# Sparse chunk attention and a gated feed-forward layer on one core: the last output tile in two halves of 256 columns, with new ranks for the order of work

## The chip, the cores and the metric

The kernel runs on one core of a Trainium2 chip. The metric is the time of one execution on the device in microseconds (us), as the median of the runs shown; lower is better. A profiled execution gives the trace: its span goes from the first to the last recorded instruction.

## The reference: what is computed

The inputs are q, k and v of shape (4, 8, 768, 64): four batches, eight heads, 768 positions, 64 features. The keys of each head are cut into 24 chunks of 32. For each query and chunk an upper bound of the scores is worked out from the chunk's smallest and largest key values; each query then attends only to the six chunks with the highest bounds, and causally within them. The result is reshaped to 3072 tokens of 512 features and goes through a gated feed-forward layer.

```
k_min, k_max = min, max of each chunk of 32 keys
ub     = sum(maximum(q * k_min, q * k_max))            # one bound per query and chunk
ub     = where(causal, ub, -1e9)
top    = six chunks with the highest ub
scores = (q @ k.T) / 8, kept where chunk in top and key <= query
attn   = softmax(scores) @ v
x      = attn reshaped to (3072, 512)
xn     = x / sqrt(mean(x*x) + 1e-6) * rms_g
out    = (silu(xn @ w_gate) * (xn @ w_val)) @ w_out    # 512 -> 1536 -> 512, float32
```

## The kernel before

**Work.** The kernel handles 16 pairs of heads, four pairs per batch. For each pair, `prep` (L487) loads q and k by SP's DMA queue (L505), transposes them on PE (L525), moves the result out of PSUM with ACT (L297) or DVE (L301), and takes each chunk's minimum and maximum on DVE (L554, L556). Queries are cast to bfloat16 into a buffer `qn` on POOL or DVE (L301). From the seventh pair on, `duo` (L778) computes the bounds for two pairs at once: matmuls on PE (`ub`, L789), evictions, transposes on PE (`up`, L811), the causal mask on DVE (L818), the eight highest values on DVE (L658), and the selection by threshold (L673, L676), which writes one column per chunk into the same `qn` buffer. Then two DMA transposes on SP (`qs<-qn`, L565), one for each head of the pair, bring queries and selection columns together into the layout that the scores read. `scores` (L851) multiplies them with the keys (`sc`, L876), adds a triangular mask (L882), takes the exponential on ACT (L893), masks on POOL (L899), multiplies with v (`av`, L912, 65 columns) and normalises on DVE (L932, L933).

When the four pairs of a batch are done for half of the rows, `norm` (L945) computes the sum of squares (ACT L960 or DVE L963), the root (DVE L973, POOL L981), scales (L989), and transposes the result by a DMA on SP (L1000) or on PE (L1011). `ffn` (L1025) runs for each batch and each half of 384 rows. For each of twelve blocks of 128 hidden features it runs four gate matmuls (L1045), the tanh on ACT (L1052), a combination on DVE (L1058), four value matmuls (L1066), and the product on DVE (`hh`, L1074). Then come three row tiles of 128 rows (`th`): each is projected by twelve matmuls of 128x512 columns into one PSUM bank (`po`, L1086), in three steps of four matmuls; the bank is copied with a factor of 0.5 into SBUF (`poE`, ACT L299 or DVE L303) and stored by a DMA of 256 KB on SP's queue (L1101).

The weights w_gate, w_val and w_out are loaded in two halves of 768 KB each by POOL's DMA queue (L445, L450), and v by the same queue (L481). In the first part of the kernel 88 dummy matmuls on zeros (L346), 48 of 512 columns and 40 of 256, stand in PE's stream.

**Order.** A planner, the class `Order` (L79), decides the order in which each engine gets its instructions while the program is built. Each step is added with the engines that may run it, a planned cost, what it waits for, and the buffers it opens and uses. Buffers come in fixed numbers: eight PSUM banks (`ps`), three output buffers (`ob`), two `qn` buffers, and so on (L235). Whenever an engine is free in the plan, it takes the ready step with the lowest rank. Where a step may run on either of two engines, the one that takes it first has it. A step's rank is the sum of the planned place of its work, an offset for its kind, and a pace times its number within the work; the offsets by kind are in the table `RANK` (L26 to L42), one for the first batch and one for the others, and the places and paces in `TIMES` (L44 to L60). In `TIMES`, `a` entries are the preparations of pairs, `l` their loads, `s` their scores, `n` the normalisations, `f` the feed-forward halves, `w` the weights. The instructions are then written out in the planned order, and each engine works off its queue in that order.

Of the kernel before, what the change touches and what calls it, by code (L numbers as in the profile page):

```python
# [8 lines left out]
FP32 = mybir.dt.float32  # L9
BF16 = mybir.dt.bfloat16  # L10
ALU = mybir.AluOpType
ACT = mybir.ActivationFunctionType
# [12 lines left out]

RANK = (  # L26
    dict(
        av=439.71, dif=-349.0, eps=-276.35, exp=56.9, kC=119.11, kE=221.89, kT=-479.5,
        kload=-91.99, kmn=-561.73, kmx=-221.73, max=-117.69, qC=120.39, qE=644.67, qN=97.14,
        qT=303.27, qX=110.23, qload=17.43, relu=-156.64, root=392.56, sc=392.96, sel=176.91,  # L30
        selC=388.0, selT=-168.59, sq=-325.5, tp=-47.15, tpE=460.17, ub=-387.44, ubE=-1000.64,
        ubm=-238.37, up=-379.03, vload=-360.06, xb=-167.37, xs=293.02,
    ),
    dict(
        av=-243.01, dif=-122.81, eps=-968.41, exp=80.0, gate=-57.45, hh=-33.27, kC=474.21,
        kE=54.78, kT=-28.02, kload=327.35, kmn=571.37, kmx=673.95, mask=-6.85, max=351.72,
        out=-338.93, po=268.25, poE=188.61, qE=-4.14, qN=444.8, qT=271.57, qX=-691.62,
        qload=314.07, relu=202.91, root=-1348.37, sc=-186.72, sel=354.08, sq=285.76, tanh=579.3,
        tg=-259.04, ub=-101.04, ubE=-390.25, ubm=307.49, up=-117.99, val=-52.48, vload=103.56,
        xT=119.23, xb=-299.83, xs=-84.52,  # L40
    ),
)  # L42

TIMES = {  # L44
# [15 lines left out]
}  # L60


# [139 lines left out]
def kernel(  # L202
# [11 lines left out]
    nc = tc.nc  # L214
    P = nc.NUM_PARTITIONS
    B, H, S, D = q.shape
# [5 lines left out]
    DM = H * D  # L222
    DFF = moe_w_gate.shape[1]
    NHT = DFF // P
# [29 lines left out]
    def add(name, engs, occ, rank, *a, **kw):  # L254
        return order.add(name, engs, occ, rank if isinstance(rank, dict) else {"": rank}, *a, **kw)
# [20 lines left out]
    def tile_of(b, shape, dtype, name):  # L276
        pool = ps if b.kind == "ps" else sb
        b.tile = pool.tile(shape, dtype, name=name, tag=f"{b.kind}{b.slot}")
        return b.tile


    def act(n):
        return 0.065 + n * 0.00083

    def dve(n):
        return 0.07 + n * 0.00104
# [40 lines left out]
    wo = const.tile([P, NHT, DM], BF16, name="wo")  # L327
# [3 lines left out]
    def make_ident(e):  # L331
# [7 lines left out]
        out=first[:], in_=ident_f[:, 0:1], func=ACT.Exp), [c_id])  # L339
# [41 lines left out]
    prev = c_id  # L381
    for n in range(4):
        prev = add("e_all", "POOL", 0.82, -80 + n, lambda e, n=n: e_step(n), [prev])
# [43 lines left out]
    def make_tri(e):  # L427
# [10 lines left out]
        out=gains[:], in_=moe_rms_g.rearrange("(o n) -> o n", o=1).to_broadcast([P, DM])),  # L438
# [15 lines left out]
    for part in range(2):  # L454
        a = add("wg", "POOL", 0.8, {f"w{part}": 1.0},
                lambda e, part=part: load_w(part, wg, moe_w_gate), load=1000000)
        b_ = add("wv", "POOL", 0.8, {f"w{part}": 1.0, "w": 1.0},
                 lambda e, part=part: load_w(part, wv, moe_w_val), load=1000000)
# [566 lines left out]
    def ffn(b, c, at, pace):  # L1025
        cols = slice(c * W, (c + 1) * W)
        hhs, hh_done = [], []
        x = [0]

        def step():  # L1030
            x[0] += 1

        def place(kind):
            return rank(at, 1, kind, x[0], pace)

        for ht in range(NHT):
            gp, vp, sg, tg, hh = Buf("ps", "ffn"), Buf("ps", "ffn"), Buf("ff"), Buf("ff"), Buf("hh")
            hs = slice(ht * P, (ht + 1) * P)
            w = c_w[ht // (NHT // 2)]
            step()  # L1040

            def gate(e, gp=gp, hs=hs):
                t = tile_of(gp, [P, W], FP32, "gp")
                for g in range(NP):
                    nc.tensor.matmul(t[:], wg[:, g, hs], XT[b].tile[:, g, cols],  # L1045
                                     start=(g == 0), stop=(g == NP - 1))

            a = add("gate", "PE", 0.652, place("gate"), gate, XTS[b][c] + [w[0]], opens=[gp], uses=[XT[b]])

            def tanh(e, gp=gp, sg=sg):  # L1050
                t = tile_of(sg, [P, W], BF16, "sg")
                nc.scalar.activation(out=t[:], in_=gp.tile[:], func=ACT.Tanh, scale=0.5)  # L1052

            a = add("tanh", "ACT", act(W), place("tanh"), tanh, [a], opens=[sg], uses=[gp])

            def mix(e, gp=gp, sg=sg, tg=tg):
                t = tile_of(tg, [P, W], BF16, "tg")
                nc.vector.scalar_tensor_tensor(out=t[:], in0=sg.tile[:], scalar=1.0,  # L1058
                                               in1=gp.tile[:], op0=ALU.add, op1=ALU.mult)

            a = add("tg", "DVE", dve(W), place("tg"), mix, [a], opens=[tg], uses=[gp, sg])

            def val(e, vp=vp, hs=hs):
                t = tile_of(vp, [P, W], FP32, "vp")
                for g in range(NP):
                    nc.tensor.matmul(t[:], wv[:, g, hs], XT[b].tile[:, g, cols],  # L1066
                                     start=(g == 0), stop=(g == NP - 1))

            step()
            d = add("val", "PE", 0.652, place("val"), val, XTS[b][c] + [w[1]], opens=[vp], uses=[XT[b]])  # L1070

            def mul(e, vp=vp, tg=tg, hh=hh):
                t = tile_of(hh, [P, W], BF16, "hh")
                nc.vector.tensor_tensor(out=t[:], in0=vp.tile[:], in1=tg.tile[:], op=ALU.mult)  # L1074

            hh_done.append(add("hh", "DVE", dve(W), place("hh"), mul, [a, d], opens=[hh], uses=[vp, tg]))
            hhs.append(hh)
        for th in range(3):
            po, ob = Buf("ps", "po"), Buf("ob")
            prev = None  # L1080
            for part in range(3):
                def proj(e, th=th, part=part, po=po):
                    if part == 0:
                        tile_of(po, [P, DM], FP32, "po")
                    for ht in range(part * 4, part * 4 + 4):
                        nc.tensor.matmul(po.tile[:], hhs[ht].tile[:, th * P:(th + 1) * P],  # L1086
                                         wo[:, ht, :], start=(ht == 0), stop=(ht == NHT - 1))

                hs = range(part * 4, part * 4 + 4)
                step()  # L1090
                prev = add("po", "PE", 0.867, place("po"), proj,
                           [prev] + [hh_done[i] for i in hs] + c_wo, opens=[po],
                           uses=[hhs[i] for i in hs])

            def out_(e, po=po, ob=ob):
                t = tile_of(ob, [P, DM], FP32, "osb")
                evict(e, t[:], po.tile[:], 0.5)

            o = add("poE", "", {"ACT": act(512), "DVE": dve(512)}, place("poE"), out_, [prev], opens=[ob], uses=[po])
            r0 = b * S + c * W + th * P  # L1100
            add("out", "SP", 0.55, place("out"), lambda e, r0=r0, ob=ob: nc.sync.dma_start(  # L1101
                out=out[r0:r0 + P, :], in_=ob.tile[:]), [o], uses=[ob])


    pairs = []
    for p in range(NPAIRS):
        c, b = make_pair(p), p // NP
# [51 lines left out]
```

## Time and profile before

| | |
|---|---|
| median of 3 runs | 316.25 us (315.89 to 316.34) |
| profiled execution, its time | 315.79 us |
| profiled execution, its span | 314.0 us |
| granted TensorE clock (mean of the run) | 1.00 |
| first PE work after the start | 1.3 us |

PE is TensorE's matmul stream, PEld its weight loads, DVE VectorE, ACT ScalarE, POOL GpSimd and SP the engine that issues most DMAs. A row of the page's list of groups reads: line, engine, operation, the tile written and the tile read, their shape, the count, then busy time in us and the mean of one in ns, then the idle time in front of them. Rows of a timeline give start and length in us. The lengths of matmuls are modelled and overlap each other; the distance between two starts is what a matmul costs in the stream. The windows view has for each stretch the length, the busy time and number of instructions for PE, PEld, DVE, ACT and POOL, the granted clock, the DMA share and GB/s. In the DMA views each digit is one of 40 equal slices, and the issues give the size and the time from issue to landing.

### The profile page before, as it was taken

What the parts mean: (1) busy time and instruction counts of PE and PEld (TensorE: products, weight loads), DVE (VectorE), ACT (ScalarE), POOL (GpSimd) and SP (SyncE); (2) the same over time, 40 slices, a digit from 0 to 9 for tenths busy, and PEclk for the clock granted to TensorE, in tenths of its full rate; (3) what the DMA queues carried; (4) which work ended last, traced back from release to release, by engine and by line L of the source; (5) the groups of instructions that cost most, each with busy time, mean ns of one, the idle gap of its engine ahead of it and who ended that gap; (6) DMA issues with size and microseconds to landing.
All of it is one profiled execution on the core that took longest, in us unless ns stands there. A gap on an engine that the chain in (4) does not pass through costs nothing.

```text
span 314.0 us, 7640 instructions
## 1 busy us (share of the span) xinstructions
PE 308.6 (98%) x2844; PEld 196.1 (62%) x2844; DVE 230.7 (73%) x654; ACT 194.4 (62%) x420; POOL 100.7 (32%) x157
## 2 busy tenths in 40 slices
PE   7999999999999999999999999999999999999995
PEld 4567877666566775666667565656666645655542
DVE  7699986888988487967986799879464663873530
ACT  5589987863475987478579654344988823333321
POOL 8666534342353564045357300001522220000000
PEclk9999999999999999999999999999999999999999
DMA  8999989989989898979934640002341045001102
GB/s 171 210 190 178 145 108 207 198 114 143 196 86 199 126 179 152 201 164 222 158 79 61 93 102 0 2 2 52 84 94 59 20 118 150 3 0 65 38 22 111
DMA packets 113301, 35.36 MB, mean 113 GB/s; under 512 B 106224, under 2 KB 110064, under 8 KB 113264
## 3 DMA queue, kind: packets, MB, share of 16 engines
q1 hardware_dynamic: 83152, 26.62, 40.9%
q0 software_dynamic: 28512, 7.87, 25.6%
q10 hardware_dynamic: 1600, 0.39, 0.6%
q8 instruction: 22, 0.36, 0.5%
q14 instruction: 15, 0.12, 0.1%
HBM read 28.57 MB, written 6.29 MB: 111 GB/s over the span
## 4 chain that ended last, share of the span: by engine, by line
PE 97%; DMA 1%; ACTq 0%; ACT 0%; issue 0%
PE gp L1045 20%; PE vp L1066 20%; PE po L1086 20%; PE sc L876 12%; PE av L912 7%; PE busy L346 4%; PE pq L525 4%; PE pk L525 3%; PE ub L789 2%; PE ub L731 2%; DMA qnat<-in_q_dram 1%; PE up L811 1%; PE sc L882 1%; PE up L755 1%; PE tp L1011 0%; ACTq L505 0%
## 5 line engine op out<-in xcount | busy, mean ns | idle before, releaser
L893 ACT ACTIVATE pt<-sc 128x512 bf16<-128x512 f32 (+2 forms) x192 | 88.4, 578 | 10.1 <-PE sc L876 5.3
L1052 ACT ACTIVATE sg<-gp 128x384 bf16<-128x384 f32 x96 | 47.7, 500 | 62.7 <-PE gp L1045 60.0
L1066 PE MATMUL vp<-xT,wv 128*128 128x384 bf16 x384 | 77.0, 326 | 0.0
L1045 PE MATMUL gp<-xT,wg 128*128 128x384 bf16 x384 | 76.2, 326 | 0.0
L1086 PE MATMUL po<-wo,hh 128*128 128x512 bf16 x288 | 69.3, 379 | 0.0
L1058 DVE SCALAR_TENSOR_TENSOR tg<-sg,gp 128x384 bf16<-128x384 bf16 x96 | 52.2, 548 | 21.7 <-ACT sg L1052 19.5
L1074 DVE TENSOR_TENSOR hh<-vp,tg 128x384 bf16<-128x384 f32 x96 | 51.8, 551 | 11.1 <-PE vp L1066 7.3
L1045 PEld LDWEIGHTS <-wg 128*128 128x128 bf16 x384 | 36.8, 98 | 24.5 <-issue 1.0
L1066 PEld LDWEIGHTS <-wv 128*128 128x128 bf16 x384 | 36.9, 98 | 24.1
L876 PE MATMUL sc<-qs,ke 128*128 128x128 bf16 (+5 forms) x420 | 51.4, 251 | 0.0
L1086 PEld LDWEIGHTS <-hh 128*128 128x128 bf16 x288 | 27.6, 98 | 27.5
L301 POOL CAST ke<-kt 64x768 bf16<-64x768 f32 x31 | 26.4, 852 | 36.9 <-ACT kt L297 17.0
L876 PEld LDWEIGHTS <-ke 128*128 128x128 bf16 (+1 forms) x420 | 30.3, 97 | 11.3 <-issue 1.6
L899 POOL TENSOR_SCALAR_AFFINE_SELECT pt<-pt 128x512 bf16<-128x512 bf16 (+1 forms) x48 | 24.4, 527 | 37.6 <-ACT pt L893 37.4
L912 PEld LDWEIGHTS <-pt 128*128 128x128 bf16 x672 | 28.8, 98 | 7.7 <-POOL ke L301 0.6
L912 PE MATMUL av<-vx,pt 128*128 128x65 bf16 x672 | 32.6, 193 | 0.0
L299 ACT ACTIVATE osb<-po 128x512 f32<-128x512 f32 x19 | 11.4, 602 | 21.4 <-PE po L1086 21.4
L346 PE MATMUL busy<-zeros 128*128 128x512 bf16 (+1 forms) x88 | 20.1, 349 | 1.3 <-DVE zeros L341 1.3
L933 DVE TENSOR_TENSOR xb<-av,rden 128x384 bf16<-128x384 f32 (+1 forms) x34 | 18.1, 534 | 1.2
L989 DVE SCALAR_TENSOR_TENSOR xs<-xb,ri,gains 128x512 bf16<-128x512 bf16 x24 | 16.9, 746 | 2.7 <-DMA xT<-xs 2.1
L301 POOL CAST qn<-qnat 128x768 bf16<-128x768 f32 x10 | 8.2, 821 | 31.9 <-DMA qs<-qn 30.7
L481 POOL DMA_DIRECT2D vx<-in_v_dram x16 | 16.8, 1052 | 4.0 <-PE av L912 2.6
(87 smaller groups left out, 303.1 us busy)
## 6 DMA issues: line engine op xcount, KB each, us to landing
out_dram<-osb SPq DMA_DIRECT2D x24, 256.0 KB, 2.2
knat<-in_k_dram SPq DMA_DIRECT2D x30, 192.0 KB, 4.3
qnat<-in_q_dram SPq DMA_DIRECT2D x30, 192.0 KB, 4.8
vx<-in_v_dram POOLq DMA_DIRECT2D x16, 192.0 KB, 4.7
wg<-in_moe_w_gate_dram POOLq DMA_DIRECT2D x2, 768.0 KB, 8.6
wv<-in_moe_w_val_dram POOLq DMA_DIRECT2D x2, 768.0 KB, 7.8
wo<-in_moe_w_out_dram POOLq DMA_DIRECT2D x2, 768.0 KB, 9.9
qs<-qn SPq DMA_TRANSPOSE x26, 3.3
```

The source lines that it names most:

```text
L301: engine[e].tensor_copy(out_, in_)
L346: nc.tensor.matmul(t[:, 0:n], zeros[:, 0:P], zeros[:, 0:n], start=True, stop=True)
L876: nc.tensor.matmul(t[:, x:x + m, :].rearrange("p a b -> p (a b)"), ke[kk, kb * P:(kb + 1) * P], qs[kk, q0 * P:(q0 + m) * P], start=not tri ...
L893: nc.scalar.activation(out=t[:, 0:nn, :], in_=sc.tile[:, 0:nn, :], func=ACT.Exp, scale=SCALE)
L899: nc.gpsimd.affine_select(out=pt.tile[:, 0:nd, :], in_=pt.tile[:, 0:nd, :], compare_op=ALU.is_ge, fill=0.0, base=0, pattern=[[0, nd], [1, ...
L912: nc.tensor.matmul(av.tile[:, qi - i0, :], pt.tile[:, x, :], VX[c.v.slot][:, hl * NT + kb, :], start=(begin and m == 0), stop=(left[0] == ...
L1045: nc.tensor.matmul(t[:], wg[:, g, hs], XT[b].tile[:, g, cols], start=(g == 0), stop=(g == NP - 1))
L1052: nc.scalar.activation(out=t[:], in_=gp.tile[:], func=ACT.Tanh, scale=0.5)
L1058: nc.vector.scalar_tensor_tensor(out=t[:], in0=sg.tile[:], scalar=1.0, in1=gp.tile[:], op0=ALU.add, op1=ALU.mult)
L1066: nc.tensor.matmul(t[:], wv[:, g, hs], XT[b].tile[:, g, cols], start=(g == 0), stop=(g == NP - 1))
L1074: nc.vector.tensor_tensor(out=t[:], in0=vp.tile[:], in1=tg.tile[:], op=ALU.mult)
L1086: nc.tensor.matmul(po.tile[:], hhs[ht].tile[:, th * P:(th + 1) * P], wo[:, ht, :], start=(ht == 0), stop=(ht == NHT - 1))
```

## The change

Two things change. First, in the last feed-forward half (batch 3, second half) the third row tile is no longer projected as one tile of 512 columns but as two of 256 columns. Each has a PSUM buffer of its own, three steps of four matmuls with 256 columns (planned cost 0.44 instead of 0.867), an eviction of 256 columns and a store of 128 KB; the store's rows are half as long. Second, every number in `RANK` and `TIMES` is another, so that the planner writes out another order for all engines, and for steps that may run on either of two engines also another share. The lines from there on move down by two (L1086 becomes L1088, L1101 becomes L1103).

In the changed order, the number of dummy matmuls is the same (88, all in the first part). Of the evictions of output tiles, ACT has 22 and DVE 3, where they had 19 and 5; there are 25 stores instead of 24 and 2306 weight-load instructions instead of 2294 in PE's program. DVE has 8 sums of squares instead of 9, and casts of queries move from POOL (10 to 8) to DVE (3 to 5). On POOL's queue the loads of w_out and v in the middle of the kernel come as w_out, w_out, v, v, v, where they came as v, w_out, v, w_out. The last two tiles on PE are the two halves, whose steps alternate.

```diff
 RANK = (
     dict(
-        av=439.71, dif=-349.0, eps=-276.35, exp=56.9, kC=119.11, kE=221.89, kT=-479.5,
...
+        av=466.73, dif=-380.72, eps=-422.75, exp=-49.4, kC=465.82, kE=55.35, kT=-458.36,
...
 TIMES = {
-    "a0": -417.11, "a1": 120.7, "a10": 211.74, "a11": -52.39, "a12": 226.13, "a13": 390.87,
...
+    "a0": -366.84, "a1": 132.4, "a10": -301.15, "a11": -280.78, "a12": 112.6, "a13": 171.18,
...
-        for th in range(3):
+        last = b == B - 1 and c == 1
+        for th, c0, cn in [(th, c0, DM >> (last and th == 2)) for th in range(3)
+                           for c0 in ((0, DM // 2) if last and th == 2 else (0,))]:
             po, ob = Buf("ps", "po"), Buf("ob")
             prev = None
             for part in range(3):
-                def proj(e, th=th, part=part, po=po):
+                def proj(e, th=th, part=part, po=po, c0=c0, cn=cn):
                     if part == 0:
-                        tile_of(po, [P, DM], FP32, "po")
+                        tile_of(po, [P, cn], FP32, "po")
                     for ht in range(part * 4, part * 4 + 4):
                         nc.tensor.matmul(po.tile[:], hhs[ht].tile[:, th * P:(th + 1) * P],
-                                         wo[:, ht, :], start=(ht == 0), stop=(ht == NHT - 1))
+                                         wo[:, ht, c0:c0 + cn], start=(ht == 0), stop=(ht == NHT - 1))
...
-                prev = add("po", "PE", 0.867, place("po"), proj,
+                prev = add("po", "PE", 0.867 if cn == DM else 0.44, place("po"), proj,
...
-            def out_(e, po=po, ob=ob):
-                t = tile_of(ob, [P, DM], FP32, "osb")
+            def out_(e, po=po, ob=ob, cn=cn):
+                t = tile_of(ob, [P, cn], FP32, "osb")
                 evict(e, t[:], po.tile[:], 0.5)
...
-                out=out[r0:r0 + P, :], in_=ob.tile[:]), [o], uses=[ob])
+                out=out[r0:r0 + P, c0:c0 + cn], in_=ob.tile[:]), [o], uses=[ob])
```

More of the change, by code (lines that the diff above doesn't have):

```diff
@@ L27 @@
     dict(
-        av=439.71, dif=-349.0, eps=-276.35, exp=56.9, kC=119.11, kE=221.89, kT=-479.5,
[L29 to L32, printed above, removed]
+        av=466.73, dif=-380.72, eps=-422.75, exp=-49.4, kC=465.82, kE=55.35, kT=-458.36,
+        kload=-100.05, kmn=-524.02, kmx=-272.62, max=-206.54, qC=257.78, qE=654.8, qN=275.73,
+        qT=529.05, qX=12.3, qload=0.57, relu=-417.11, root=416.88, sc=450.99, sel=18.52,
+        selC=468.92, selT=-164.48, sq=-287.14, tp=109.6, tpE=391.45, ub=-307.85, ubE=-1094.17,
+        ubm=-73.2, up=-317.03, vload=-423.9, xb=-192.06, xs=156.67,
     ),
     dict(
[L35 to L40, printed above, removed]
+        av=-136.54, dif=-25.64, eps=-1081.06, exp=140.8, gate=-101.16, hh=-181.84, kC=554.23,
+        kE=88.0, kT=11.55, kload=300.77, kmn=615.67, kmx=590.94, mask=-156.54, max=409.75,
+        out=-160.07, po=360.72, poE=184.39, qE=-57.45, qN=239.45, qT=248.62, qX=-905.32,
+        qload=292.54, relu=385.33, root=-1275.79, sc=-251.68, sel=314.94, sq=325.53,
+        tanh=712.19, tg=-281.52, ub=-209.58, ubE=-381.85, ubm=458.61, up=-72.05, val=-72.19,
+        vload=295.95, xT=55.23, xb=-371.76, xs=-157.23,
     ),
@@ L1081, in ffn @@
             for part in range(3):
-                def proj(e, th=th, part=part, po=po):
+                def proj(e, th=th, part=part, po=po, c0=c0, cn=cn):
                     if part == 0:
-                        tile_of(po, [P, DM], FP32, "po")
+                        tile_of(po, [P, cn], FP32, "po")
                     for ht in range(part * 4, part * 4 + 4):
                         nc.tensor.matmul(po.tile[:], hhs[ht].tile[:, th * P:(th + 1) * P],
-                                         wo[:, ht, :], start=(ht == 0), stop=(ht == NHT - 1))
+                                         wo[:, ht, c0:c0 + cn], start=(ht == 0), stop=(ht == NHT - 1))
                 hs = range(part * 4, part * 4 + 4)
                 step()
-                prev = add("po", "PE", 0.867, place("po"), proj,
+                prev = add("po", "PE", 0.867 if cn == DM else 0.44, place("po"), proj,
                            [prev] + [hh_done[i] for i in hs] + c_wo, opens=[po],
                            uses=[hhs[i] for i in hs])
-            def out_(e, po=po, ob=ob):
-                t = tile_of(ob, [P, DM], FP32, "osb")
+            def out_(e, po=po, ob=ob, cn=cn):
+                t = tile_of(ob, [P, cn], FP32, "osb")
                 evict(e, t[:], po.tile[:], 0.5)
-            o = add("poE", "", {"ACT": act(512), "DVE": dve(512)}, place("poE"), out_, [prev], opens=[ob], uses=[po])
+            o = add("poE", "", {"ACT": act(cn), "DVE": dve(cn)}, place("poE"), out_, [prev], opens=[ob], uses=[po])
             r0 = b * S + c * W + th * P
-            add("out", "SP", 0.55, place("out"), lambda e, r0=r0, ob=ob: nc.sync.dma_start(
-                out=out[r0:r0 + P, :], in_=ob.tile[:]), [o], uses=[ob])
+            add("out", "SP", 0.55, place("out"), lambda e, r0=r0, ob=ob, c0=c0, cn=cn: nc.sync.dma_start(
+                out=out[r0:r0 + P, c0:c0 + cn], in_=ob.tile[:]), [o], uses=[ob])
     pairs = []
```

28 rows, old and new, of the table TIMES are left out of this document.

## The prediction

> **What bounds the kernel now.** I read the page first, the busy shares and then the chain that ended last; after that the waits of PE, a table by windows, and the last ten microseconds in order of time.
>
> ```profile
> span 314.0 us, 7640 instructions
> PE 308.6 (98%) x2844; PEld 196.1 (62%) x2844; DVE 230.7 (73%) x654; ACT 194.4 (62%) x420; POOL 100.7 (32%) x157
> ...
> PE 97%; DMA 1%; ACTq 0%; ACT 0%; issue 0%
> ...
> L1086 PE MATMUL po<-wo,hh 128*128 128x512 bf16 x288 | 69.3, 379 | 0.0
> ```
> ```profile
> PE busy L346 <- DVE zeros L341: 1.3, 1, 1.3
> PE pq L525 <- DMA qnat<-in_q_dram: 0.3, 1, 0.3
> ```
> ```profile
> 10.00:310.00 300.00, 299.97 (x2810) 191.96 (x2792) 224.03 (x636) 187.72 (x412) 92.59 (x134) 1.00 0.67 110
> ```
>
> PE is busy for 98% of the span, the chain lies on it for 97%, and the whole list of its waits is 1.6 us, all at the start. Between 10 and 310 us it is busy for 299.97 us at a granted clock of 1.00. So the time is: a start of about 1.3 us, one stream of matmuls, and a tail. No other engine is near its limit (DVE 73%). A change can shorten the stream's work, shorten the tail, or open holes in the stream. The 379 ns of a projection matmul are a modelled length with a drain in it. What it costs in the stream is the distance from one start to the next, read from the end of the chain (start, length, what):
>
> ```profile
> 300.74 9.51 PE po L1086 x44
> 310.25 0.03 ACTq L299
> 310.27 0.04 issue
> 310.32 0.60 ACT osb L299
> ```
>
> 44 matmuls in 9.51 us are 0.216 us each. The tail after 310.25 is an eviction of 0.60 us on ACT, the store, and the finish. The store's landing and the shape of its traffic, from 302 to 314 us in 40 slices of 0.3 us:
>
> ```profile
> DMA  0000000000005986960000000000039949900000
> GB/s 0 0 0 0 0 0 0 0 0 0 0 0 205 382 287 239 382 253 0 0 0 0 0 0 0 0 0 0 0 116 369 369 164 369 348 14 0 0 0 0
> ...
> out_dram<-osb SPq DMA_DIRECT2D x4, 256.0 KB, 2.0
> ```
>
> Four stores of 256 KB go in two bursts of six slices; a store moves data for three slices, 0.9 us, and lands 2.0 us after its issue. With the issue at 310.32 + 0.60 = 310.92 it lands at about 312.9, and 1.1 us of finish lead to 314.0. The profiled execution took 315.79 us, so 1.74 us lie around the span, which I carry over unchanged.
>
> **The change part by part.** *The split.* For the last row tile, 24 matmuls of 256 columns replace 12 of 512. What 256 columns cost in the stream is shown by the dummy matmuls (start, length, line, xcount):
>
> ```profile
> 49.44 1.04 PE L346 MATMUL busy<-zeros 128*128 128x256 bf16 x8
> 50.32 0.82 PE L525 MATMUL pq<-ident_f,qnat 128*128 128x128 f32 x6
> ```
>
> Eight in 50.32 − 49.44 = 0.88 us are 0.110 us each. The split adds 24 × 0.110 − 12 × 0.216 = **+0.05 us**. The stream also loads 12 more weight tiles, at 98 ns a load by these rows:
>
> ```profile
> L1086 PEld LDWEIGHTS <-hh 128*128 128x128 bf16 x288 | 27.6, 98 | 27.5
> ```
> ```profile
> 244.69 0.66 PE L912 MATMUL av<-vx,pt 128*128 128x65 bf16 x16
> 245.19 0.39 PE L876 MATMUL sc<-qs,ke 128*128 128x128 bf16 x4
> ```
>
> I cost these loads at nothing because the attention product (second fence) needs a new weight tile for each matmul of 65 columns, and 16 of those start within 245.19 − 244.69 = 0.50 us, 31 ns each: loads overlap even there. If that cover were gone, they would cost 12 × 0.098 = 1.18 us.
>
> [...]
>
> *The tail.* The changed order interleaves the two halves in parts of four matmuls, so the halves finish 4 × 0.110 = 0.44 us apart; both are evicted by ACT. ACT's nearest forms to a 256-column float32 eviction, and the present one:
>
> ```profile
> L299 ACT ACTIVATE osb<-po 128x512 f32<-128x512 f32 x19 | 11.4, 602 | 21.4 <-PE po L1086 21.4
> ...
> L297 ACT ACTIVATE ubs<-ub 96x256 f32<-96x256 f32 x6 | 2.2, 373 | 3.7 <-PE ub L731 3.7
> ...
> L893 ACT ACTIVATE pt<-sc 128x256 bf16<-128x256 f32 x2 | 0.9, 428 | 0.0
> ```
>
> The last eviction falls from 602 to between 373 and 428 ns: **−0.22 us** by the nearer row in type (float32 out), −0.17 at the other end. Either is under 0.44, so the first half is off ACT before the second arrives. The last store carries 128 KB. Its 128 rows stay 128 rows, each half as long, so the 0.9 us of moving data fall by 0.45 if bytes count and by nothing if rows count. I take **−0.30**, nearer the end where bytes count, and keep 0 and −0.45. The store of the first half is issued 0.44 us ahead of it and asks SP for nothing else.
>
> *The new ranks.* They reorder every queue, but PE's work outside the split is unchanged: the same matmul groups and the same 88 dummies, all in the first part of the stream. Order can therefore win only holes. The clearest two in the first order:
>
> ```profile
> 38.59 0.27 PE L346 MATMUL busy<-zeros 128*128 128x256 bf16 x1
> 38.89 0.38 PE L876 MATMUL sc<-qs,ke 128*128 128x128 bf16 x4
> ...
> 39.39 0.27 PE L346 MATMUL busy<-zeros 128*128 128x256 bf16 x1
> 39.65 0.38 PE L876 MATMUL sc<-qs,ke 89*128 89x128 bf16 x4
> ```
>
> A dummy covers 0.11 us, but the next start is 0.30 and 0.26 later: holes of 0.19 and 0.15 us. If both go, −0.35; if waits of the same size come in their place and as much again, +0.4. I take **0**: nothing in these rows says which order has fewer. What an order can lose beyond that is the slower rival, below.
>
> *Sum:* +0.05 − 0.22 − 0.30 + 0 = **−0.47 us** on the profiled 315.79, so 315.3. The median of the three runs, 316.25, is 0.46 above the profiled run; carried over, the forecast is **315.8 us**, 0.15% faster.
>
> **The rivals.** *Slower: transposed queries land late behind a weight load.* The first scores of the second group of heads read qs, which SP transposes by DMA:
>
> ```profile
> L565 SPq DMA_TRANSPOSE qs<-qn x2: 1674/1699/1724, 45.8 to 47.6; - x2
> ...
> DMA to landing us min/median/max: 6.0/6.5/7.0
> ```
> ```profile
> 57.82 0.93 PE L876 MATMUL sc<-qs,ke 89*128 89x128 bf16 x8
> ```
> ```profile
> 49.24 0.80 POOL L445 DMA_DIRECT2D wg<-in_moe_w_gate_dram  x1
> ```
> ```profile
> q0 software_dynamic: 330, 0.51, 107.0%
> ...
> wg<-in_moe_w_gate_dram POOLq DMA_DIRECT2D x1, 768.0 KB, 10.2
> ...
> qs<-qn SPq DMA_TRANSPOSE x2, 6.5
> ```
>
> The transposes are issued at 45.8 and 47.6 and land by 53.6; the read is at 57.8, a margin of 4.2 us. They are slow because of POOL's loads: from 47 to 50 us only POOL's queue moved packets (the row of q0), though both transposes were already issued. In the changed order the bound's transposes on PE (L811) stand 2.2 us of matmul starts later in PE's queue, and DVE has one more normalisation pair and one more sum of squares ahead of the threshold that the query cast needs:
>
> ```profile
> L933 DVE TENSOR_TENSOR xb<-av,rden 128x384 bf16<-128x384 f32 x30 | 16.7, 557 | 1.0
> ...
> L963 DVE CUSTOM_DVE_ANT_0 junk<-xb 128x512 bf16<-128x512 bf16 x9 | 6.1, 688 | 0.2
> ...
> L932 DVE RECIPROCAL rden<-av 128x6 f32<-128x6 f32 x30 | 5.7, 190 | 11.8 <-PE av L912 11.8
> ```
>
> These are 0.19 + 0.56 + 0.69 = 1.44 us, with the 2.2 about 3.7 us, so the issues fall at about 49.5 and 51.3. The half that the first scores read is the second one there. With the old 6.0 to landing it arrives at 57.3, a margin of 0.5: no stall. But the second half of w_gate is issued at about 49.2, no longer behind the transposes but ahead of at least one. If the transpose waits out that load, 49.2 + 0.8 + the 7.5 to 10.2 us that half weights take to land is 57.5 to 60.2:
>
> ```profile
> wv<-in_moe_w_val_dram POOLq DMA_DIRECT2D x1, 768.0 KB, 7.5
> ```
>
> So PE stalls for 0 to 2.6 us. I price it at 1.5, a little over the middle because what follows the scores needs them, and get 315.8 + 1.5 = **317.3**. It decides from the point where a transpose takes over 6.5 us from issue. Against it: transposes alone land in 2.7 us, as in the window from 214 to 235 us, and other matmuls stand close behind the scores.
>
> ```profile
> qs<-qn SPq DMA_TRANSPOSE x8, 2.7
> ```
>
> [...]
>
> *Slower: half-width matmuls pay their own weight loads.* Then the 1.18 us above come on the path: 315.8 + 1.18 = 317.0. The 31 ns of the 65-column matmuls speak against it.
>
> *The change does not do what it says:* the half store takes as long as a whole one, because rows count or because it moves behind the first half's. Only the eviction is won: 316.25 + 0.05 − 0.22 = 316.1. For it: the number of rows is unchanged.
>
> *Faster than forecast:* bytes count in full and both early holes go: +0.05 − 0.22 − 0.45 − 0.35 = −0.97, so 315.3.
>
> **How the numbers follow.** The forecast (315.8, its own range 315.5 to 316.2) has 45%; the store that wins nothing (316.1) 13%; faster (315.3) 18%; late queries (317.3) 21%; weight loads 3%. A measurement of this kernel can tell about 0.2% from no change, 0.63 us: faster is below 315.62, slower above 316.88. Of the forecast's 45% I put 15 below 315.62, because the sum's two bounds of the store straddle it, 30 within; of the faster rival all 18; the store rival within, 13; of the late queries 19 above and 2 within; the weight loads 3 above. That gives faster 33%, within 45%, slower 22%. The range of 8 in 10 reaches from 315.1, just under the faster rival, to 317.2, which takes in the late queries' cheaper half.
>
> **What would show it.** In the changed kernel's profile: the last projection groups in 256 columns at 0.11 us a start (step one); a last eviction of 128x256 of 0.37 to 0.43 us; a last store of 128 KB that lands 1.55 to 2.0 us after its issue; PE's busy time between 10 and 310 us within 0.4 us of the whole. Scores waiting for qs near 58 us, with the transposes landing over 6.5 us after their issue, would show the slower rival. The prediction is wrong if PE's list of waits has a line over 0.5 us that is not at the start, or if the two halves' starts lie 0.16 us or more apart.

## The result, and the profile after

| | before | changed |
|---|---|---|
| median, all runs | 316.16 us (8 runs, 315.89 to 316.42) | 320.4 us (8 runs, 317.1 to 324.3) |
| ratio to before | | **1.0086**, 95% interval 1.0062 to 1.0111 |
| profiled execution, time and span | 315.79 and 314.0 us | 318.26 and 316.6 us |

The change makes the kernel slower, by about 0.9%, and it makes it uneven: the runs of before lie within 0.6 us, those of the changed kernel within 7.2. The ratio leaves out three runs of 323.7 to 324.3 us with a granted clock of 0.988 to 0.989.

The page of the changed kernel answers the same questions as that of before. The rows are the span, the busy times, and the shares of the chain that ended last, by engine and by line.

```profile
span 316.6 us, 7643 instructions
...
PE 308.7 (98%) x2839; PEld 197.8 (62%) x2856; DVE 234.0 (74%) x656; ACT 193.7 (61%) x420; POOL 101.8 (32%) x156
...
PE 89%; DMA 5%; DVE 2%; ACT 1%; POOL 1%; issue 1%; ACTq 0%
PE po L1088 19%; PE vp L1066 19%; PE gp L1045 18%; PE sc L876 11%; PE av L912 6%; DMA qs<-qn 5%; PE busy L346 4%; PE pk L525 4%; PE pq L525 3%; PE ub L789 2%; PE ub L731 2%; PE up L811 1%; PE sc L882 1%; DVE selq L687 0%; ACT qs L297 0%
```

PE has the same work (308.7 us) in a span that is 2.5 us longer (316.55 against 314.05, which the pages round). The busy shares alone say nothing: 98% in both. The chain says it: a DMA, `qs<-qn`, holds 5% of it, where before had PE for 97%. The list of PE's waits (us in total, times, longest) names the same transfer:

```profile
PE sc L876 <- DMA qs<-qn: 1.9, 2, 1.3
PE busy L346 <- DVE zeros L341: 1.3, 1, 1.3
```

Two timelines, of PE, show the two places:

```profile
57.51 0.81 PE L1066 MATMUL vp<-xT,wv 128*128 128x384 bf16 x4
59.61 1.04 PE L876 MATMUL sc<-qs,ke 89*128 89x128 bf16 x10 [1.29 <-DMA qs<-qn]
```
```profile
89.67 0.81 PE L1045 MATMUL gp<-xT,wg 128*128 128x384 bf16 x4
91.11 1.05 PE L876 MATMUL sc<-qs,ke 89*128 89x128 bf16 x10 [0.64 <-DMA qs<-qn]
```

Four matmuls of 384 columns fill 0.65 us of the stream, as in the row `61.57 0.65 PE vp L1066 x4` of the chain, so the scores could have started at 58.16 and 90.32. They started 1.45 and 0.79 us later, 2.24 us in all. The chain in order of time gives, for each place, when the transpose that they waited for was issued, and how long it took:

```profile
51.12 8.44 DMA qs<-qn
59.56 0.04 issue
59.61 1.04 PE sc L876 x10
```
```profile
83.93 7.14 DMA qs<-qn
91.07 0.05 issue
91.11 1.05 PE sc L876 x10
```

In between, POOL's queue moves other transfers. At the first place the timelines of POOL and SP, then the queues' packets from 52 to 56 us (packets, MB, share of 16 engines), read:

```profile
50.24 0.79 POOL L445 DMA_DIRECT2D wg<-in_moe_w_gate_dram  x1
```
```profile
49.77 2.58 SPq L565 DMA_TRANSPOSE qs<-qn  x2
```
```profile
q0 software_dynamic: 361, 0.55, 100.2%
...
q1 hardware_dynamic: 34, 0.00, 1.2%
...
qs<-qn SPq DMA_TRANSPOSE x1, 8.4
```

The load of w_gate is issued between the two transposes. The second transpose is issued behind it, and for four microseconds its queue, q1, moves 34 packets against 361. At the second place it is the same with three loads of v, issued from 75.7 us:

```profile
75.67 3.07 POOL L481 DMA_DIRECT2D vx<-in_v_dram  x3 [0.20 <-issue]
```
```profile
q0 software_dynamic: 3090, 0.44, 217.1%
...
q1 hardware_dynamic: 1, 0.00, 0.0%
...
qs<-qn SPq DMA_TRANSPOSE x2, 7.5
```

This second fence is the window from 82 to 85 us; in it one packet of q1 moves. That the loads of v are what holds the transposes there is read from these rows alone; it was not tried by itself.

The tail did what the split says. The last pieces of the chain:

```profile
306.18 6.68 PE po L1088 x40
312.86 0.03 ACTq L299
312.88 0.04 issue
312.93 0.39 ACT osb L299
313.32 0.04 issue
313.37 0.38 ACT osb L299
```

The last eviction takes 0.38 us instead of 0.60, the two evictions start 0.44 us apart, and from the last eviction's end (313.75) to the end of the span (316.55, by the page 316.6) are 2.8 us where before had 314.0 − 310.92 = 3.1. So the tail gave some time back, and the stream itself ends later than the spans tell: PE was done at 310.25 us before and is done at 313.3 us now (310.82 + 2.46 by its timeline), 3.05 us later. The two waits are 2.24 of these; the other 0.8 us are small losses elsewhere, of which PE's list of waits names three of 0.2 us each.

### The profile page after: what moved, and what is told of

It reads as the page before. It is cut to its first block, busy times and chain, and to the rows that moved or that the text cites. A ratio compares the mean times of both kernels' runs of the same rounds, so it can differ in the third digit from the quotient of the medians.

```text
span 316.6 us, 7643 instructions
## 1 busy us (share of the span) xinstructions
PE 308.7 (98%) x2839; PEld 197.8 (62%) x2856; DVE 234.0 (74%) x656; ACT 193.7 (61%) x420; POOL 101.8 (32%) x156
## 4 chain that ended last, share of the span: by engine, by line
PE 89%; DMA 5%; DVE 2%; ACT 1%; POOL 1%; issue 1%; ACTq 0%
PE po L1088 19%; PE vp L1066 19%; PE gp L1045 18%; PE sc L876 11%; PE av L912 6%; DMA qs<-qn 5%; PE busy L346 4%; PE pk L525 4%; PE pq L525 3%; PE ub L789 2%; PE ub L731 2%; PE up L811 1%; PE sc L882 1%; DVE selq L687 0%; ACT qs L297 0%
## 5 line engine op out<-in xcount | busy, mean ns | idle before, releaser
L893 ACT ACTIVATE pt<-sc 128x512 bf16<-128x512 f32 (+3 forms) x192 | 87.0, 596 | 8.1 <-PE sc L876 7.5
L1066 PE MATMUL vp<-xT,wv 128*128 128x384 bf16 x384 | 75.2, 326 | 0.0
L1045 PE MATMUL gp<-xT,wg 128*128 128x384 bf16 x384 | 74.5, 326 | 0.0
L1088 PE MATMUL po<-wo,hh 128*128 128x512 bf16 (+1 forms) x285 | 65.5, 370 | 0.7
L1058 DVE SCALAR_TENSOR_TENSOR tg<-sg,gp 128x384 bf16<-128x384 bf16 x96 | 51.2, 548 | 18.5 <-ACT sg L1052 16.9
L876 PE MATMUL sc<-qs,ke 128*128 128x128 bf16 (+5 forms) x420 | 52.5, 251 | 2.1 <-DMA qs<-qn 1.9
L1066 PEld LDWEIGHTS <-wv 128*128 128x128 bf16 x384 | 36.4, 98 | 24.2 <-issue 1.2
L1088 PEld LDWEIGHTS <-hh 128*128 128x128 bf16 x300 | 28.6, 98 | 27.7
L912 PEld LDWEIGHTS <-pt 128*128 128x128 bf16 x672 | 30.0, 98 | 6.9 <-POOL pt L899 0.3
L912 PE MATMUL av<-vx,pt 128*128 128x65 bf16 x672 | 34.0, 193 | 0.2 <-POOL pt L899 0.2
L299 ACT ACTIVATE osb<-po 128x512 f32<-128x512 f32 (+1 forms) x22 | 12.7, 579 | 25.5 <-PE po L1088 25.5
L658 DVE MAX8 m<-ubm 128x8 f32<-128x8 f32 (+2 forms) x192 | 16.7, 162 | 0.0
```

The lines of the kernel that those rows point to most:

```text
L876: nc.tensor.matmul(t[:, x:x + m, :].rearrange("p a b -> p (a b)"), ke[kk, kb * P:(kb + 1) * P], qs[kk, q0 * P:(q0 + m) * P], start=not tri ...
L893: nc.scalar.activation(out=t[:, 0:nn, :], in_=sc.tile[:, 0:nn, :], func=ACT.Exp, scale=SCALE)
L912: nc.tensor.matmul(av.tile[:, qi - i0, :], pt.tile[:, x, :], VX[c.v.slot][:, hl * NT + kb, :], start=(begin and m == 0), stop=(left[0] == ...
```

## The experiments

Three theories stood at the start. **A**: the loss comes from transposed queries that land late, because the half that the scores read first is now transposed second, and late, behind POOL's loads; the split is worth what was forecast. **B**: the new order loses small times in many places. **C**: the split itself costs time. All ratios are to before on the same chip; their 95% intervals stand in brackets.

**The two parts of the change, apart.** The first kernel has the tables of before and the split, the second the new tables and the old loop over row tiles.

```diff
+        last = b == B - 1 and c == 1
+        for th, c0, cn in [(th, c0, DM >> (last and th == 2)) for th in range(3)
+                           for c0 in ((0, DM // 2) if last and th == 2 else (0,))]:
```

> The ranks of before with the split of the last tile: the order is that of before up to the last tile. Theory A (the loss comes from queries that are transposed late, and the split is worth what was forecast): 0.47 us under before, 315.7 us, no wait of PE for qs, a last eviction near 0.41 us and a last store that lands 1.7 us after its issue. Theory C (half-width matmuls or a second store cost time): at or above before, 316.2 to 317.4 us.

```diff
-        last = b == B - 1 and c == 1
+        for th in range(3):
```

> The new ranks without the split: the last tile is one of 512 columns again. Theory A: all of the loss stays and the tail's gain goes, so 0.3 to 0.6 us over the changed kernel's undisturbed runs, which lie from 317.1 to 321, and the waits of PE for qs near 59 and 90 us stay. Theory C: the loss is gone, 316.2 us.

Split alone: **0.9981** [0.9973, 0.9990], median 315.37 us (314.96 to 316.01) against 315.96, 0.59 under before. Its profile shows what half-width matmuls cost, each with its own weight load:

```profile
308.83 1.58 PE L1088 MATMUL po<-wo,hh 128*128 128x256 bf16 x13
```

One such matmul is 0.27 us long (272 ns for the 24 of the changed kernel), so twelve distances from start to start take 1.58 − 0.27 = 1.31 us, 0.109 us each, as forecast. Order alone: **1.0096** [1.0064, 1.0129], from 316.81 to 323.89 us. Its profile is that of its fastest run and has a wait of PE for qs of 1.0 us near 58 us; the wait near 90 us, which was expected to stay, is not in it. Theory C falls; the whole loss, and the scatter, come with the order.

**The order of the two halves.** Nothing is moved but the two transposes of each pair on SP's queue; the instructions of PE, DVE and ACT stay as they are.

```diff
     done = order.run(PLACE)
+    turns = [i for i, s in enumerate(done) if s.name == "qX"]
+    for i, j in zip(turns[0::2], turns[1::2]):
+        done[i], done[j] = done[j], done[i]
```

> The changed kernel with nothing moved but the two DMA transposes of each pair of heads on SP's queue: the half that the scores read first goes first. Theory A: PE's waits for qs of 1.3 and 0.6 us go, 316.2 to 316.5 us, and the runs lie within 0.5 us of each other, as those of before do. Theory B (the new order loses small times in many places, and the queries are only the visible part): at most 0.7 us better than the changed kernel, 317 to 318 us and still spread.

Measured: **0.9994** [0.9983, 1.0005], 315.6 us (315.22 to 317.06). PE's list of waits has no row for qs any more:

```profile
PE busy L346 <- DVE zeros L341: 1.3, 1, 1.3
PE vp L1066 <- DVE tg L1058: 0.3, 1, 0.3
PE av L912 <- POOL pt L899: 0.2, 1, 0.2
```

The changed kernel's median was 4.2 us over before; with two exchanged DMAs per pair it is 0.4 under before (315.96), and most of the scatter is gone: 1.8 us from the fastest to the slowest run instead of 7.2, though not the 0.5 that was expected. What is left for theory B is small and open: by the ratios the kernel with the split alone is 0.13% better, 0.4 us, but the two intervals overlap. The last two rows above are the waits that the stream still has, near 155 and 162 us; which instruction of the new order causes them was not tried.

**Lateness without the change.** Two factors, each alone and both together, in the kernel before: the threshold step of the fifth pair some 3 us later, and the halves exchanged.

```diff
     done = order.run(PLACE)
+    def shift(step, anchor):
+        done.remove(step)
+        done.insert(done.index(anchor) + 1, step)
+
+    def find(name, *keys):
+        return [s for s in done if s.name == name and all(k in s.keys for k in keys)]
+
+    last = find("eps", "n0.0")[0]
+    for s in find("qX", "a4")[::-1] + find("sel", "a4"):
+        shift(s, last)
```

> The kernel before, with the threshold step of the fifth pair of heads (and its two transposes, in their old order) moved on DVE behind the two normalisations, two sums of squares and the mean that followed it, about 3.1 us later. The half that the scores read first still goes first. Theory A (lateness and the order of the two halves together make the loss): the first transpose is issued near 49 us and lands by 56 at the latest, ahead of the read at 57.8, and the second by about 60, when its scores come; no wait for qs over 0.3 us and at most 0.2% over before, 315.8 to 316.6 us. Theory A2 (lateness alone is enough): the loss of the next kernel, 317 us and more.

With the exchange of the experiment above added to it:

> The same delay in the kernel before, and the two transposes of every pair in the other order, the half that is read first behind the other. Theory A: PE waits for qs at the scores near 58 us for 0.5 to 2.5 us, 316.6 to 319 us, with a spread of over 1 us among the runs. If the loss of the changed kernel has another cause: as the kernel without the swap, no wait.

And the exchange alone:

> The kernel before with only the order of the two transposes of every pair exchanged, and no delay. Theory A: the later transpose lands by 53.6 us and the read is at 57.8, so no wait and the time of before, within 0.2%. Theory A3 (the order of the halves alone is enough): 316.8 us or more.

| kernel before with | ratio | wait of PE for qs near 58 us |
|---|---|---|
| late threshold | 0.9997 [0.9985, 1.0008] | none |
| exchanged halves | 1.0002 [0.9992, 1.0011] | none |
| both | **1.0091** [1.0058, 1.0124] | 2.8 us |

The kernel with both has four runs, from 317.86 to 319.99 us. The rows behind the table's last line, the transposes' issue and landing and PE's wait, in the kernel with both:

```profile
L565 SPq DMA_TRANSPOSE qs<-qn x2: 1222/1231/1240, 48.5 to 49.8; - x2
...
DMA to landing us min/median/max: 7.4/9.1/10.7
```
```profile
60.62 1.05 PE L876 MATMUL sc<-qs,ke 89*128 89x128 bf16 x10 [2.81 <-DMA qs<-qn]
```

And in the kernel with the late threshold alone:

```profile
L565 SPq DMA_TRANSPOSE qs<-qn x2: 1232/1260/1287, 48.8 to 50.0; - x2
...
DMA to landing us min/median/max: 7.1/8.3/9.5
```

The transfers are slow in both. The second of the two lands at 60.5 with both factors and at 59.5 with the delay alone, after the read is due at 57.9; it costs nothing where it carries the half that is read later. Each factor alone is free, both together make a loss of the same size (1.0091, where the order alone had 1.0096) in a kernel that has neither the changed tables nor the split. That is theory A, shown from the other side.

**The load that holds the transpose.** In the changed kernel, the second half of w_gate is moved on POOL's queue, once earlier, once later; the transposes keep their order.

```diff
+    shift(find("wg", "w1")[0], find("wv", "w0")[0])
```

> The changed kernel with the load of the second half of w_gate moved on POOL's queue from behind the root of the first normalisation to right behind the first half of w_val, some 5 us earlier; the transposes keep their order. Theory A, with the weight load as what the second transpose waits for: its packets are through before the second transpose is issued at 51.1 us or soon after, so the wait near 59 us falls from 1.3 to between 0 and 0.5 us, and that near 90 us stays: 316.5 to 317.3 us. If the queue of transposes itself is slow (theory A without the weight load), the wait near 59 us stays at 1.3 us or grows.

```diff
+    shift(find("wg", "w1")[0], find("root", "n0.1")[0])
```

> The changed kernel with the load of the second half of w_gate moved on POOL's queue behind the root of the second normalisation, near 56.6 us, so that no weight load is under way when the two transposes are issued at 49.8 and 51.1. Theory A with the weight load as what holds the transposes: both land within 5 us of their issue, so the wait of PE for qs near 59 us is gone; instead the gate matmuls near 63 us wait for w_gate, up to 2 us. If the transposes are slow by themselves or behind other traffic of their own queue: the wait near 59 us stays at 1 us or more.

Earlier: **1.0042** [1.0024, 1.0060], 317.24 us (316.3 to 320.25). The median is as expected, but the profiled run, the slowest of the twelve, still waits 1.75 us for qs: the two weight loads now move one behind the other, and both transposes come behind them, as the packets from 50 to 54 us show:

```profile
q0 software_dynamic: 475, 0.71, 112.0%
```

No other data queue moves a packet in these four microseconds. The expectation for the wait was wrong: an earlier issue of the load did not clear the queue in time. It was wrong on the wait near 90 us too, which was to stay and is not in this profile. Later: 1.0075 [1.0028, 1.0122], three runs. There no load of w_gate is under way. That of the first half of w_val still is when the first transpose is issued at 49.4 us, but it is almost through: POOL's queue moves 122 packets from 49 to 50 us, then 12 and 8 in the next two. The landing and the row of PE's waits that is new read:

```profile
DMA to landing us min/median/max: 4.5/4.7/5.0
```
```profile
PE gp L1045 <- DMA wg<-in_moe_w_gate_dram: 1.3, 1, 1.3
```

The second transpose lands after 4.5 us instead of 8.4 (the first takes 5.0 in both), the wait for qs is gone, and the gate matmuls wait for the weights instead. The load is what the second transpose waits out; it is also needed soon, so moving it only moves the wait.

The kernel before has the opposite case. There the same load was issued at 49.24 us, behind both transposes (45.8 and 47.6). From 51 to 53 us it was the load that stood almost still, while SP's queue, q1, moved; the transposes landed at 52.8 and 53.6:

```profile
q1 hardware_dynamic: 1688, 0.42, 105.7%
q0 software_dynamic: 53, 0.06, 15.9%
```

So neither queue has the upper hand as such. At the places looked at here, what was issued first went first, whichever queue it stood in: that fits the changed kernel, the kernel before, and the earlier and the later load. The reason is not shown.

**What the split is worth, term by term.** With the ranks of before, the tile is projected and evicted in two halves but stored as one, from slices of one buffer; then it is cut in three.

```diff
-            po, ob = Buf("ps", "po"), Buf("ob")
+            po = Buf("ps", "po")
+            if c0 == 0:
+                ob, moved = Buf("ob"), []
...
+            moved.append(o)
+            if c0 + cn < DM:
+                continue
```

> The ranks of before, with the last tile projected and evicted in two halves, but stored whole, as 256 KB after the second eviction. It keeps the eviction's gain and drops the store's. By the forecast's terms: 0.3 us over the kernel with two half stores, 315.7 us, with 3.1 us from the last eviction's end to the end of the span, as before. If half a store takes as long as a whole one: the same time as the kernel with two half stores, 315.4 us.

```diff
+        ends = [(2, 0, 256), (2, 256, 128), (2, 384, 128)] if last else [(2, 0, DM)]
+        for th, c0, cn in [(0, 0, DM), (1, 0, DM)] + ends:
```

> The ranks of before, with the last tile in three pieces of 256, 128 and 128 columns. If the tail goes by bytes: the last eviction falls from 0.38 to about 0.27 us (0.60 at 512 columns and 0.38 at 256 put on a line), the last store of 64 KB lands 0.1 to 0.2 us sooner than the 128 KB one, 24 matmuls of 128 columns cost 0.02 us more than 12 of 256: 0.2 to 0.3 us under the kernel with two halves, 315.1 us. If the store goes by rows, whose number stays 128: 0.1 us under it. If more and smaller pieces cost more than they save: at or over it, 315.4 us.

Whole store: 0.9993 [0.9984, 1.0002], 315.87 us, and 3.1 us from the last eviction's end (310.89 + 0.38) to the end of the span (314.4), as before; with half stores it was 313.6 − 310.88 = 2.7. So by the profiles the eviction's gain is 0.2 us, the store's 0.4; the times of the runs (0.9993 against 0.9981 for half stores) say the same, but with intervals that overlap. Three pieces: 1.0005 [0.9996, 1.0014], no gain. Its chain shows why:

```profile
309.33 0.60 ACT osb L299
309.93 0.02 issue
309.95 2.05 DMA out_dram<-osb
312.00 0.02 issue
312.02 0.04 ACTq L299
312.06 0.04 issue
312.10 0.28 ACT osb L299
```

There are three output buffers. By the timeline ACT was free from 311.16 us (310.88 + 0.28), but the last eviction waited until 312.0 for a store to leave its buffer. The same three pieces in slices of one buffer, with the two halves in one buffer beside them:

```diff
             def out_(e, po=po, ob=ob, c0=c0, cn=cn):
+                if ob.tile is None:
+                    tile_of(ob, [P, DM], FP32, "osb")
+                evict(e, ob.tile[:, c0:c0 + cn], po.tile[:], 0.5)
...
+                out=out[r0:r0 + P, c0:c0 + cn], in_=ob.tile[:, c0:c0 + cn]), [o], uses=[ob])
```

> The three pieces of 256, 128 and 128 columns again, now in slices of one output buffer, each stored on its own, so that the last eviction needs no buffer that an earlier store still reads. If that wait was all that the pieces lost: the last eviction starts within 0.1 us of the last matmul's end, takes 0.28 us, and the time is 0.1 to 0.3 us under the kernel with two halves in its own run, about 315.1 us. If more stores cost by themselves: at or over the two halves.

> The control for the three pieces: the two halves of the change, the ranks of before, in slices of one output buffer with a store each. Expected as the kernel with the split alone: 0.5 us under before, 315.5 us, 2.7 us from the last eviction's end to the end of the span.

Three pieces 0.9988 [0.9979, 0.9997], two halves 0.9987 [0.9976, 0.9997], on the same chip: the wait is gone, but a third piece wins nothing that can be told, against the 0.1 to 0.3 us that were expected. The version to keep is the order of before with the last tile in two halves, 0.1 to 0.2% better than before (0.9987 and 0.9981).

## Why the prediction was wrong

- **The bound, the split, the tail: right.** Split alone was forecast at −0.47 us and measured −0.59; the two halves in one buffer measured 315.53 against 316.0, −0.47. The half-width matmuls cost 0.109 us each where 0.110 was forecast. The eviction's −0.22 was exact (0.60 to 0.38). The store's −0.30 was somewhat small: by the profiles 3.1 to 2.7 is −0.4, near the end where bytes count. The rival "half-width matmuls pay their own loads" is out. So is "the half store wins nothing", by the profiles: in the changed kernel, the split alone and the two halves in one buffer the half stores land after 1.7 to 1.8 us (medians), the whole ones after 2.0.
- **The new ranks taken at 0: the step that failed.** The likeliest case let the transposed queries arrive "at 57.3, a margin of 0.5: no stall", by the old 6.0 us to landing. The sign that it named for being wrong, a line of over 0.5 us in PE's list of waits, is there with 1.9. The issue times were right (49.5 and 51.3 forecast, 49.8 and 51.1 measured), with one slip: the transposes of the bound that come later on PE are those of L755 (the last at 42.3 us before, at 44.8 now), not L811. The read fell due at 58.16, so a landing of up to 7.0 us would have done, where the prediction had 6.5. It took 8.4, as the rival described it. The rival's mechanism and its place were right. That its price came so near (1.5 forecast, 1.45 in the profile) is partly luck: it was picked inside 0 to 2.6 us, whose upper end should have been 60.2 − 57.8 = 2.4, and the same wait was 1.0, 1.75 and 2.81 us in the profiles of order alone, the early load and both factors. The facts for preferring the rival were in the views of before: the old landings of 6.0 and 7.0 us had been read where w_gate's load came behind both transposes, and in the changed order it came between them. A duration that was measured in front of a load is no estimate for a place behind it.
- **What the rival's price left out.** A second place of the same kind, at 90 us, where three loads of v stand ahead of the transposes (0.79 us in the profile of the changed kernel, none in those of order alone and of the early load); the small losses elsewhere, some 0.8 us in that profile; and the scatter from run to run, with a lowered clock in some runs, below. These make 317.3 too low, and with it the range's upper end of 317.2.
- **Not weighed: the halves' order.** The prediction states that the half read first is the second one in the changed order, and uses it only for a time. It is one of the two factors: with the halves put right, the rest of the new order costs 0.4 us by the ratios, or nothing that the intervals can tell. That lies within the bounds that the prediction gave it (−0.35 to +0.4).
- **What the other queue had ahead.** By the windows above the transposes got almost nothing beside a load that was issued ahead of them (34 packets against 361 in four microseconds; 1 against 3090 in three), and the load got almost nothing beside transposes that were ahead of it (53 against 1688 in two). Why is not shown; but an estimate with a fair share for each queue would have been wrong here.

## What to carry to other kernels

Where a consumer reads several transfers in a known order, issue them in that order: here it cost nothing that could be measured, and it turned a wait for the second transfer into slack (0.9994 instead of 1.0086, with no wait for qs left). When a change moves a transfer, list what stands ahead of it in the other queues at its new time, and take its duration from a place that had the same things ahead of it; here a margin of half a microsecond, counted with 6.0 us to landing, became a stall of 1.45 us when the transfer took 8.4. A stream that is 98% busy cannot be improved by a new order by more than its holes, but it can lose by late transfers: two of them cost 2.24 us in the profile here.

## What the runs showed of the hardware

In one profiled run the granted clock fell to 0.50 behind a stall, and the run lost more than the stall. It is the run with the early w_gate load: PE waited 1.75 us, and the windows around and after it (length, busy times and counts by engine, granted clock, DMA share, GB/s) read:

```profile
58.00:60.00 2.00, 0.48 (x3) 0.19 (x2) 2.00 (x5) 0.36 (x1) 0.00 (x0) 1.00 1.36 176
60.00:61.00 1.00, 0.76 (x10) 0.64 (x10) 0.86 (x2) 0.34 (x1) 0.66 (x1) 0.98 1.34 223
61.00:64.00 3.00, 3.00 (x12) 1.39 (x10) 0.00 (x0) 2.49 (x6) 1.51 (x3) 0.50 1.36 217
64.00:65.00 1.00, 1.00 (x12) 0.74 (x11) 0.43 (x1) 0.15 (x1) 0.00 (x0) 0.81 1.03 164
```

From 61 to 64 us PE ran at half clock, 0.50, with 12 matmuls. At 0.50 for 3 us and 0.81 for one, that is 1.7 us lost beside the 1.75 of the wait; over a span of 318.5 us it is a mean clock of 0.995, which is what the run shows. This run took 320.25 us where the others of the kernel lie between 316.3 and 318.0. In the changed kernel's three longest runs, a mean clock of 0.988 to 0.989 over some 322 us is at most 3.9 us of the 7.5 to 8.1 that they took over before. The rest is by this estimate time without work, more than in the profiled run; no trace of such a run was kept, so where they lost it is not shown. Nor does a long wait always bring the clock down: the kernel with both factors waited 2.81 us in its profile, and its clock stayed at 1.00:

```profile
58.00:60.00 2.00, 0.00 (x0) 0.00 (x0) 1.32 (x3) 0.34 (x1) 0.00 (x0) 1.00 1.40 121
60.00:61.00 1.00, 0.38 (x7) 0.38 (x8) 0.00 (x0) 0.00 (x0) 0.28 (x1) 1.00 1.35 206
61.00:64.00 3.00, 3.00 (x29) 2.00 (x27) 1.64 (x3) 2.94 (x7) 2.31 (x4) 1.00 1.36 217
```

So between these two runs, 1.75 us with a clock of 0.50 behind it and 2.81 us with 1.00, the length of the wait alone does not decide it. What does is not shown.
